# Later loads of k and v, rounding steps in turns for the second channel weight, and a closed joint, in a fused attention and mixer kernel

## The chip, the cores and the metric

The kernel runs on one core of a Trainium2 chip. Its engines are PE (TensorE, matmuls), DVE (VectorE), ACT (ScalarE), POOL (GpSimd) and SP (SyncE, which here issues nearly all DMAs). The metric is device time in microseconds, the median of several runs. Before the change it is 807.17 us (four runs, 806.99 to 807.58).

## The reference

All inputs of the attention are float32; the four weights of the mixer arrive in double precision and are rounded to float32 on the chip.

```python
# q, k, v: 8 batches, 8 heads, 576 rows, 64 columns
kv = einsum('bhsd,bhse->bhde', k, v)
out = einsum('bhsd,bhde->bhse', q, kv)
rms = sqrt(mean(out * out, axis=-1, keepdims=True) + 1e-06)
x = out / rms * g_norm                  # then to (8, 576, 512)
# mixer; w_tok1 576x256, w_tok2 256x576, w_ch1 512x1536, w_ch2 1536x512
h = maximum(x^T @ w_tok1, 0) @ w_tok2
u = x + h^T
h2 = maximum(u @ w_ch1, 0) @ w_ch2
result = u + h2
```

## The kernel before

The work has two parts. The **first pass** makes u = x + h for all eight batches, and rounds the weights on the side. The **second part** computes the channel mixing of u in nine groups of 512 rows (eight groups of the first 512 rows of a batch, and a ninth of the 64 remaining rows of each). Between the two u goes through DRAM (`u_dram`).

**First pass.** It works on pairs of batches, four pairs in all. Its order is written out by hand, as lists of names: `start` (attention of pair 0), `middle` (attention of pair 1, mixing of pair 0), `steady` twice (attention of pairs 2 and 3, mixing of pairs 1 and 2) and `last` (mixing of pair 3). `play` (L1059) runs a list from left to right, and each engine's queue follows that order. The names: `kv` products of k and v and `e` their eviction; `l00` to `l11` the loads of k and v for the next pair (`load`, L132: each issues two DMAs for k and two for v, on SP, into one of four pairs of buffers); `lq` the load of q; `a` the attention product of a chunk, `g` the product with g_norm (DVE), `q` the squares (ACT), `t` their sums (DVE), `m`, `r`, `i` the mean, root and inverse of the norm (DVE, ACT, DVE), `s` and `p` the scaling by the inverse (ACT or POOL); `h` the first token product, `z` the copy of x to PSUM as the start of a second token product, `u` the second token product with its eviction and the store of u. The two digits tell side or chunk and half.

A plain number in a list, such as `2`, runs that many steps of the **rounding** of the channel weights. A block of such a weight goes through eight functions: `fetch` (DMA of raw double words), `scale` (ACT), and six on DVE: clamp, shift, sign, power, lower and `both` (the sum of the two halves). `get_ch1` makes eight blocks of 128x768, `get_ch2` six of 128x1024. `stream` (L1048) puts the blocks behind each other, so that the six DVE steps of a block follow one another; the scale of the next block hangs on a block's fifth step (lower) and the fetch of the fourth block ahead on its sixth. Raw data has four buffers, the intermediate `part` one.

**Second part.** Both channel products use Strassen's scheme: seven products of halves in place of eight. In groups 1 to 8 it is applied twice over, with sums of weight blocks (`sums`) made once and kept in DRAM; `fetch_sums` brings them in, three ahead. Group 0 is done apart, with one level: `channel1_once` (matmuls into `ps_v`), then `channel2_once` (L703, into `ps_w`), while DVE makes the sums of the weights between its reads; `weave` spreads these over the products. The seven products of `channel2_once` stand in the order first, sixth, second, seventh, fifth, fourth, third. Fourth and third are read by DVE into the group's result `xg` and then stored.

Groups 1 to 8 are planned by place: `products[place]` holds one inner product, `beside[place]` what is issued after it. `outer` (L763) is one of the seven outer products, with seven inner ones at the places of `PLACE` (first at 0, sixth at 3, fifth at 4). After its first inner product ACT copies the bank `ps_a` to a bank `ps_c` of the pool "c" (two banks, `read_first`, L791), and the sixth product, which adds to `ps_a`, comes after that copy.

At the joint of group 0 and group 1 two matmuls whose result is not used stand around the first inner product (L1221 to 1224).

Of the kernel before, what the change touches and what calls it, by code (L numbers as in the profile page):

```python
# [11 lines left out]
F32 = mybir.dt.float32  # L12
# [7 lines left out]
def kernel(  # L20
# [33 lines left out]
    P = 128  # L54
    B, S, DM = k.shape
# [7 lines left out]
    NC, NF, NTOK = DM // P, DCH // P, DTOK // P  # L63
# [3 lines left out]
    FQ = FH // 2  # L67
# [31 lines left out]
    w_ch1 = consts.tile([P, 4, 4, FQ], F32, name="w_ch1")  # L99
# [6 lines left out]
    def do(f, *a, **kw):  # L106
        return lambda: f(*a, **kw)

    late = {}
# [454 lines left out]
    def fetch_x(g, i):  # L564

        if g < NG:
            if i == 0:
                xg[g] = late["xg"].tile([P, J, DM], F32, name="xg")
            dma(xg[g][:, ts(i, 2)], u_dram[g].rearrange("(t p) e -> p t e", p=P)[:, ts(i, 2)])
# [11 lines left out]
    blocks, blocks_dram = {}, {}  # L581
# [37 lines left out]
    def m_psum(shape, name):  # L619
        return late["m"].tile(shape, F32, name=name, tag="m")  # L620
# [82 lines left out]
    def channel2_once(g):  # L703

        shape = [P, 2, DH]
        x = xg[g]
        quarter = lambda i, j: x[:, 2 * i:2 * i + 2, ts(j, DH)]

        def product(n, ps, start, stop):
            for p in range(2):  # L710
                for s in range(NS):
                    matmul(ps[:, p], lhsT=late["once"][n - 1][:, s, p], rhs=w2_of(n)[:, s],
                           start=(start and p == 0 and s == 0), stop=stop,
                           skip_group_check=True)

        p1, p6, p7, p5 = (m_psum(shape, f"ps_w{n}") for n in (1, 6, 7, 5))
        t1, u2, u3 = (r_tile() for _ in range(3))

        def first():
            product(1, p1, True, False)  # L720
            copy(t1, p1)

        def sixth():
            product(6, p6, True, True)
            tensor_add(u2, p6, t1)

        def seventh():
            product(7, p7, True, False)
            tensor_add(u3, p7, u2)
            tensor_add(quarter(0, 1), quarter(0, 1), u2)  # L730
            tensor_add(quarter(1, 0), quarter(1, 0), u2)

        def fifth():
            product(5, p5, True, False)
            tensor_add(u3, p5, u3)
            tensor_add(quarter(1, 1), quarter(1, 1), u3)

        def second():
            product(2, p1, False, True)
            tensor_add(quarter(0, 0), p1, quarter(0, 0))  # L740

        def fourth():
            product(4, p7, False, True)
            tensor_add(quarter(1, 0), p7, quarter(1, 0))
            store(g, xg, 1)

        def third():
            product(3, p5, False, True)
            tensor_add(quarter(0, 1), p5, quarter(0, 1))
            store(g, xg, 0)  # L750

        return [first, sixth, second, seventh, fifth, fourth, third]
# [7 lines left out]
    def put(place, *steps):  # L760
        beside[place] += steps

    def outer(place, size, mul, to, base=None, act=copy, onto=False):  # L763

        banks, t = {}, {}

        def product(n, name, start, stop):
            if start:
                banks[name] = m_psum([P, size], f"ps_{name}")
            mul(n, banks[name], start, stop)

        def temp(n, bufs):
            t[n] = late["tmp"].tile([P, FQ], F32, name=n, tag=n, bufs=bufs)[:, :size]
            t[n] = fit(t[n])
            return t[n]

        def fit(flat):
            return flat if size == P else flat.rearrange("p (w t) -> p w t", w=W)

        def read(o, i, j):

            if base:
                tensor_add(o, fit(banks["a"]), base(i, j))
            else:
                copy(o, fit(banks["a"]))

        def read_first():  # L791
            banks["c"] = late["c"].tile([P, DM], F32, name="ps_c")[:, :size]
            read(fit(banks["c"]), 0, 0)

        def write(i, j, name, n):
            tensor_add(to(i, j), fit(banks[name]), to(i, j) if onto else t[n])

        def put_on(i, j, n):
            if onto:
                tensor_add(to(i, j), to(i, j), t[n])  # L800

        def take(i, j, name, act):
            if onto:
                tensor_add(to(i, j), banks[name], to(i, j))
            else:
                act(to(i, j), fit(banks[name]))

        def at(n, name, start, stop, *steps):
            def all_of():
                product(n, name, start, stop)  # L810
                for step in steps:
                    step()

            products[place + PLACE[n]] = all_of

        at(1, "a", True, False, read_first)
        at(6, "a", False, False, lambda: read(temp("u2", 2), 0, 1))
        at(5, "b", True, False)
        at(7, "a", False, False, lambda: read(temp("u3", 1), 1, 1))
        at(2, "c", False, True, lambda: take(0, 0, "c", act))  # L820
        put(place + PLACE[7] + (1 if onto else 2), do(put_on, 1, 1, "u3"), do(write, 1, 1, "b", "u3"))
        at(4, "a", False, True, lambda: take(1, 0, "a", copy) if onto else read(to(1, 0), 1, 0))
        put(place + PLACE[4], do(put_on, 0, 1, "u2"))
        at(3, "b", False, True)
        put(place + PLACE[3] + 1, do(write, 0, 1, "b", "u2"))
# [213 lines left out]
    def weave(body, fill):  # L1039
        done = 0  # L1040
        for n, step in enumerate(body):
            step()
            upto = len(fill) * (n + 1) // len(body)
            while done < upto:
                fill[done]()
                done += 1

    def stream(blocks, ahead=4):  # L1048


        steps = [blocks[0][1]]
        for n, block in enumerate(blocks):
            steps += block[2:]
            for at, m, k in ((-2, n + 1, 1), (-1, n + ahead, 0)):
                if m < len(blocks):
                    steps[at] = do(lambda *fs: [f() for f in fs], steps[at], blocks[m][k])
        return iter(steps)

    def play(lines, after={}, **stages):  # L1059

# [2 lines left out]
        for name in " ".join(lines).split():  # L1063
# [5 lines left out]
            else:  # L1069
# [6 lines left out]
    channel = ([get_ch1(c, f) for f in range(2) for c in range(NC)]  # L1076
               + [get_ch2(f) for f in range(NF // 2)])
# [20 lines left out]
    for block in tok1[2:] + tok2:  # L1098
# [11 lines left out]
        "h010 t21 m2 r2", "a30 g30 q30 i2 p20", "a31 g31 q31 t30", "h011 t31 m3 r3 p21", "a40 i3 p30 g40 q40 p31",  # L1110
        "h012 h013 t40 m4 r4 w21 i4 s40 lq0 l10 l11"]
    middle = [
        "kv00 e00 w31 w22 w23 w24", "h10 w25 w26 w27 f1 -lq1 l00 w32 w33 w34", "kv01 e01 l01 w41 w35 w36 w37",
        "h11 f2 w42 w43 w44", "hr w45 w46 w47 f3", "a0 q00 g01 q01 g00 t00 t01", "u0 z2 1", "u1 1",
        "a1 q10 g11 q11 g10 t10 t11 m0 r0", "u2 i0 1", "kv10 e10 z4 s00", "u3 1 s01", "kv11 e11 1",
        "u4 1 z6", "a2 q20 g21 q21 g20 s10", "u5 t20 t21 2", "a4 q40 g41 q41 g40 lq0 l10 l11", "u6 t40 t41 2",
        "a3 q30 g31 q31 g30 lq1 s11", "u7 t30 t31 m2 r2 1 i2 p20 p21 s30", "u8 1 s31"]

    def steady(n0, n1):
        return [  # L1120
            "kv00 l00 e00 1 -s40", "h00 3", "kv01 l01 e01 1", "h01 3", f"a0 q00 g01 q01 g00 {n0}",
            "h10 1 t00 t01 2", "h11 4", "hr 2 z2", "a1 q10 g11 q11 g10 1", "kv10 l10 e10 t10 t11 m0 r0 1",
            "u0 i0 1", "kv11 l11 e11", "u1 1 s00", "u2 z4 1", "a2 q20 g21 q21 g20", "u3 s01 t20 t21",
            "u4 z6 1", "a4 q40 g41 q41 g40 lq0", "u5 s10 t40 t41 1", "a3 q30 g31 q31 g30 lq1",
            "u6 s11 t30 t31 m2 r2 1 i2 p20 p21 s30", f"u7 1 s31 {n1}", "u8 2"]

    attentions = [attention(0, ((0,), (1,), (2,), (3,), (4,)))]
# [3 lines left out]
    mixings.append(token_mixing(B // 2 - 1, range(2, 9), (0, 1)))  # L1131
    more = {f"w{n}{k}": f for n, b in enumerate(tok1 + tok2) for k, f in enumerate(b)}
    more |= {f"f{n}": b[0] for n, b in enumerate(channel)}
    rounding = stream(channel)

    def keep_warm(n):

# [8 lines left out]
    for n in range(1, B // 2 - 1):  # L1146
        play(steady(*((3, 1), (0, 0))[n - 1]), attention=attentions[n + 1], mixing=mixings[n], before=attentions[n],
             rounding=rounding)
# [7 lines left out]
    first = ExitStack()  # L1156
# [46 lines left out]
    turns, loads = blocks1[1::2], blocks1[2::2]  # L1203
    n = len(sums1) // 3
# [8 lines left out]
             lambda: [f() for f in outer_u(1)], lambda: [f() for f in inner_u(1, 0, 7)]]  # L1213
    extra += [lambda: None] * (len(channel2_once_steps := channel2_once(0)) - len(extra))
    body = [step for pair in zip(channel2_once_steps, extra) for step in pair]
    weave(body, lasts + [f for fs, _ in inner2 for f in fs] + [f for _, f in inner1])
    fetch_x(1, 0)
    fetch_x(1, 1)


    for place in range(2):  # L1221
        t = late["c"].tile([P, DM], F32, name="ps_c")
        step = do(matmul, t[:, :FQ], lhsT=w_ch1[:, 0, 0, :P], rhs=w_ch1[:, 0, 0], start=True, stop=True)
        put(place, step) if place else step()
    for n, (_, f) in enumerate(inner2):
        put(8 + n, f)
    for g in range(1, NG):
# [42 lines left out]
```

## Time and profile before

The profile is of one execution, with times in microseconds from the start of its span.

| what | us |
|---|---|
| median of four runs | 807.17 |
| the profiled execution | 806.5 |
| its span | 804.7 |
| PE busy | 788.0 |
| DVE busy | 683.2 |
| ACT busy | 302.1 |
| POOL busy | 79.6 |
| `start` | 0 to 45 |
| `middle` | 45 to 79 |
| `steady`, first | 79 to 122.5 |
| `steady`, second | 122.5 to 167.6 |
| `last` | 167.6 to 199.3 |
| group 0, first channel product | 199.3 to 235.6 |
| group 0, second channel product | 235.6 to 271.9 |
| groups 1 to 8 | 273.9 to 804.7 |

In a line of a timeline the first number is the start, the second the length, then the engine, the line of the code, the operation, and output and input with shapes; "x4" means four instructions drawn together, and square brackets hold the idle time before them and what ended it. SPq is SP's DMA issue. The granted clock of TensorE was 0.999 over the span.

### The profile page before, as it was taken

The numbers are of one execution on the slowest core, as the hardware profiler recorded it, in microseconds if no ns is written. First come the engines' busy times: TensorE is split into PE (matmuls) and PEld (weight loads), VectorE is DVE, ScalarE is ACT, GpSimd is POOL, SyncE is SP. The second block draws the span as 40 slices with busy tenths as digits, with TensorE's granted clock in tenths as the row PEclk, the third lists the DMA queues.
The fourth block names the chain that finished last, engine by engine and source line by source line (L and its number), as shares of the span: only waits on it lengthen the run. The fifth ranks groups of instructions, "written<-read, shape, count | busy, mean of one in ns | idle before, by whom it ended". The sixth has DMA issues, their size and how long they took to land.

```text
span 804.7 us, 17651 instructions
## 1 busy us (share of the span) xinstructions
PE 788.0 (98%) x7012; PEld 694.0 (86%) x7012; DVE 683.2 (85%) x1308; ACT 302.1 (38%) x838; POOL 79.6 (10%) x75
## 2 busy tenths in 40 slices
PE   6999999999999999999999999999999999999997
PEld 6645545444888899999999999999999999999997
DVE  4688999999886978978987997897898899799687
ACT  1357585664210134234234234332424323423331
POOL 1210101010000021012003003001101200300300
PEclk9999999999999999999999999999999999999999
DMA  9999997436458567468457647738836855863642
GB/s 292 329 345 346 333 358 297 157 128 205 156 176 294 193 216 226 139 214 271 149 201 242 194 155 258 232 118 263 263 121 217 262 166 183 250 201 124 217 147 83
DMA packets 97346, 175.51 MB, mean 218 GB/s; under 512 B 7024, under 2 KB 54128, under 8 KB 97264
## 3 DMA queue, kind: packets, MB, share of 16 engines
q1 hardware_dynamic: 95584, 172.65, 65.7%
q10 hardware_dynamic: 1680, 1.74, 0.7%
q8 instruction: 55, 0.90, 0.5%
q14 instruction: 27, 0.22, 0.1%
HBM read 137.79 MB, written 36.57 MB: 217 GB/s over the span
## 4 chain that ended last, share of the span: by engine, by line
PE 83%; DVE 8%; DMA 4%; ACT 4%; issue 1%; SPq 0%; ACTq 0%; DVEq 0%
PE ps_a L127 37%; PE ps_b L127 19%; PE ps_c L127 9%; PE ps_v L127 5%; PE ps_w L127 5%; PE ps_u L127 3%; PE ps_h L127 3%; DMA v_in<-in_v_dram 2%; ACT x L475 2%; DVE x L421 1%; DVE ms L442 1%; DMA raw<-in_moe_w_ch_dram 1%; DMA k_in<-in_k_dram 1%; PE ps_o L127 1%; DVE part L187 1%; ACT sq L425 1%
## 5 line engine op out<-in xcount | busy, mean ns | idle before, releaser
L124 ACT COPY u<-ps_a 128x128 f32<-128x128 f32 (+1 forms) x160 | 56.1, 351 | 156.5 <-PE ps_a L127 156.5
L118 POOL TENSOR_TENSOR v<-v,v 128x384 f32<-128x384 f32 (+1 forms) x48 | 61.4, 1299 | 532.6 <-ACT v L124 492.8
L127 PE MATMUL ps_b<-uT,sums 128*128 128x128 f32 x672 | 86.2, 276 | 0.0
L127 PEld LDWEIGHTS ps_b<-uT,sums 128*128 128x128 f32 x672 | 80.7, 192 | 0.1
L118 DVE TENSOR_TENSOR v<-v,v 128x768 f32<-128x768 f32 (+1 forms) x86 | 79.4, 931 | 1.1
L127 PE MATMUL ps_a<-uT,w_ch 128*128 128x128 f32 x576 | 78.8, 275 | 0.0
L124 ACT COPY ps_c<-ps_a 128x128 f32<-128x128 f32 (+1 forms) x80 | 26.9, 336 | 129.5 <-PE ps_a L127 129.5
L118 DVE TENSOR_TENSOR v<-ps_b,u 128x384 f32<-128x384 f32 x112 | 61.6, 550 | 12.5 <-PE ps_b L127 10.7
L127 PEld LDWEIGHTS ps_a<-uT,w_ch 128*128 128x128 f32 x576 | 71.5, 192 | 0.4
L127 PE MATMUL ps_u<-h,w_tok 128*128 128x512 f32 (+1 forms) x160 | 68.0, 608 | 1.0 <-DVE w_tok L118 0.5
L127 PE MATMUL ps_h<-x,w_tok 128*128 128x512 f32 (+1 forms) x160 | 65.8, 604 | 0.0
L118 DVE TENSOR_TENSOR uT<-uT 128x512 f32<-128x512 f32 (+4 forms) x103 | 63.0, 628 | 0.8
L127 PE MATMUL ps_a<-uT,w 128*128 128x128 f32 x432 | 60.0, 275 | 0.0
L127 PEld LDWEIGHTS ps_a<-uT,w 128*128 128x128 f32 x432 | 54.0, 192 | 0.0
L127 PEld LDWEIGHTS ps_h<-x,w_tok 128*128 128x128 f32 (+1 forms) x160 | 25.9, 189 | 31.0 <-issue 28.3
L118 DVE TENSOR_TENSOR sv<-v 128x384 f32<-128x384 f32 x80 | 43.4, 550 | 10.4 <-ACT v L121 10.4
L127 PEld LDWEIGHTS ps_u<-h,w_tok 128*128 128x128 f32 (+1 forms) x160 | 24.5, 178 | 31.3 <-issue 24.9
L121 ACT ACTIVATE v<-v 128x384 f32<-128x384 f32 (+1 forms) x86 | 42.5, 527 | 23.0 <-DVE v L118 22.5
L118 DVE TENSOR_TENSOR xg<-xg,r 128x512 f32<-128x512 f32 x74 | 49.9, 685 | 0.7
L475 ACT ACTIVATE x<-x,inv 128x64 f32<-128x64 f32 x184 | 46.1, 337 | 9.6 <-DVE inv L461 9.6
L127 PE MATMUL ps_a<-sums,sv 128*128 128x128 f32 x336 | 47.0, 276 | 0.0
L127 PE MATMUL ps_a<-uT,sums 128*128 128x128 f32 x336 | 46.8, 275 | 0.0
(134 smaller groups left out, 1575.3 us busy)
## 6 DMA issues: line engine op xcount, KB each, us to landing
sums<-sums SPq DMA_DIRECT2D x112, 576.0 KB, 4.1
qT<-in_q_dram SPq DMA_DIRECT2D x8, 1152.0 KB, 9.7
xt<-u_dram SPq DMA_DIRECT2D x36, 256.0 KB, 3.7
blocks<-y SPq DMA_DIRECT2D x72, 128.0 KB, 2.6
uT<-blocks SPq DMA_DIRECT2D x36, 256.0 KB, 4.8
xg<-u_dram SPq DMA_DIRECT2D x18, 512.0 KB, 5.1
k_in<-in_k_dram SPq DMA_DIRECT2D x16, 512.0 KB, 9.2
u_dram<-x SPq DMA_DIRECT2D x16, 512.0 KB, 4.6
```

The source lines that it names most:

```text
L118: keep(engine.tensor_tensor(out=o, in0=a, in1=b, op=op))
L121: keep(nc.scalar.activation(o, a, AF.Relu))
L124: keep(nc.scalar.copy(o, a))
L127: keep(nc.tensor.matmul(*a, **kw))
L187: keep(nc.vector.scalar_tensor_tensor(out=part[0], in0=raw()[..., 0], scalar=2.0 ** -52, in1=part[0], op0=ALU.mult, op1=ALU.mult))
L421: keep(nc.vector.tensor_mul(x, bank[c, h], g_sb.to_broadcast([P, number(c), D])))
L425: keep(nc.scalar.activation(sq[c, h], bank[c, h], AF.Square))
L442: keep(nc.vector.tensor_reduce(stats_of(c)[0][:, h], sq[c, h], axis=AX.X, op=ALU.add))
L475: keep(nc.scalar.activation(x[:, k, h], x[:, k, h], AF.Copy, scale=inv[:, k, h]))
```

## The change

The lists get new places for the eight load steps of `middle` and `steady` (four names in each), one more rounding step at the end of `middle`, and `stream` gets an argument `turns`. Blocks below that number (the eight of the first channel weight) go as before. For the later ones (the second channel weight) the first three steps of a block alternate with the last three of the block before; the next block's scale hangs on the second step (shift), and the fetch of the fourth block ahead on the fifth (lower).

At the joint the two unused matmuls go. The last product of `channel2_once`, `third`, is taken out of the woven list and issued after the first inner product of group 1, followed by the two fetches of group 1's u. Two of the four PSUM banks of `channel2_once` now come from the pool "c", which `read_first` uses.

```diff
-        p1, p6, p7, p5 = (m_psum(shape, f"ps_w{n}") for n in (1, 6, 7, 5))
+        p1, p6 = (m_psum(shape, f"ps_w{n}") for n in (1, 6))
+        p7, p5 = (late["c"].tile(shape, F32, name="ps_c", tag="c") for _ in range(2))
...
-            banks["c"] = late["c"].tile([P, DM], F32, name="ps_c")[:, :size]
+            banks["c"] = late["c"].tile([P, DM], F32, name="ps_c", tag="c")[:, :size]
...
-    def stream(blocks, ahead=4):
+    def stream(blocks, turns, ahead=4):
+        def all_of(*fs):
+            return do(lambda: [f() for f in fs])
         steps = [blocks[0][1]]
-        for n, block in enumerate(blocks):
-            steps += block[2:]
-            for at, m, k in ((-2, n + 1, 1), (-1, n + ahead, 0)):
-                if m < len(blocks):
-                    steps[at] = do(lambda *fs: [f() for f in fs], steps[at], blocks[m][k])
-        return iter(steps)
+        second = []
+        for n in range(len(blocks)):
+            _, _, *first = blocks[n]
+            if n + 1 < len(blocks):
+                k = 1 if n >= turns else 4
+                first[k] = all_of(first[k], blocks[n + 1][1])
+            if n + ahead < len(blocks):
+                k = 4 if n >= turns else 5
+                first[k] = all_of(first[k], blocks[n + ahead][0])
+            if n < turns:
+                steps += first
+            else:
+                pairs = zip(first[:3], second or [None] * 3)
+                steps += [f for pair in pairs for f in pair if f]
+                second = first[3:]
+        return iter(steps + second)
...
     middle = [
-        "kv00 e00 w31 w22 w23 w24", "h10 w25 w26 w27 f1 -lq1 l00 w32 w33 w34", "kv01 e01 l01 w41 w35 w36 w37",
-        "h11 f2 w42 w43 w44", "hr w45 w46 w47 f3", "a0 q00 g01 q01 g00 t00 t01", "u0 z2 1", "u1 1",
+        "kv00 e00 w31 w22 w23 w24", "h10 w25 w26 w27 f1 -lq1 w32 w33 w34", "kv01 e01 w41 w35 w36 w37",
+        "h11 f2 w42 w43 w44", "hr l00 w45 w46 w47 f3", "a0 q00 g01 q01 g00 t00 t01", "u0 z2 1", "u1 l01 1",
         "a1 q10 g11 q11 g10 t10 t11 m0 r0", "u2 i0 1", "kv10 e10 z4 s00", "u3 1 s01", "kv11 e11 1",
-        "u4 1 z6", "a2 q20 g21 q21 g20 s10", "u5 t20 t21 2", "a4 q40 g41 q41 g40 lq0 l10 l11", "u6 t40 t41 2",
-        "a3 q30 g31 q31 g30 lq1 s11", "u7 t30 t31 m2 r2 1 i2 p20 p21 s30", "u8 1 s31"]
+        "u4 1 z6", "a2 q20 g21 q21 g20 s10", "u5 t20 t21 2", "a4 q40 g41 q41 g40 lq0", "u6 t40 t41 2 l10",
+        "a3 q30 g31 q31 g30 lq1 s11", "u7 t30 t31 m2 r2 1 i2 p20 p21 s30", "u8 2 l11 s31"]
     def steady(n0, n1):
         return [
-            "kv00 l00 e00 1 -s40", "h00 3", "kv01 l01 e01 1", "h01 3", f"a0 q00 g01 q01 g00 {n0}",
-            "h10 1 t00 t01 2", "h11 4", "hr 2 z2", "a1 q10 g11 q11 g10 1", "kv10 l10 e10 t10 t11 m0 r0 1",
-            "u0 i0 1", "kv11 l11 e11", "u1 1 s00", "u2 z4 1", "a2 q20 g21 q21 g20", "u3 s01 t20 t21",
-            "u4 z6 1", "a4 q40 g41 q41 g40 lq0", "u5 s10 t40 t41 1", "a3 q30 g31 q31 g30 lq1",
+            "kv00 e00 1 -s40", "h00 3", "kv01 e01 1", "h01 3", f"a0 q00 g01 q01 g00 l00 {n0}",
+            "h10 1 t00 t01 2", "h11 l01 4", "hr 2 z2", "a1 q10 g11 q11 g10 1", "kv10 e10 t10 t11 m0 r0 1",
+            "u0 i0 1", "kv11 e11", "u1 1 s00 l10", "u2 z4 1", "a2 q20 g21 q21 g20", "u3 s01 t20 t21",
+            "u4 z6 1 l11", "a4 q40 g41 q41 g40 lq0", "u5 s10 t40 t41 1", "a3 q30 g31 q31 g30 lq1",
             "u6 s11 t30 t31 m2 r2 1 i2 p20 p21 s30", f"u7 1 s31 {n1}", "u8 2"]
...
-    rounding = stream(channel)
+    rounding = stream(channel, 2 * NC)
...
     body = [step for pair in zip(channel2_once_steps, extra) for step in pair]
+    behind = body.pop(-2)
     weave(body, lasts + [f for fs, _ in inner2 for f in fs] + [f for _, f in inner1])
-    fetch_x(1, 0)
-    fetch_x(1, 1)
-    for place in range(2):
-        t = late["c"].tile([P, DM], F32, name="ps_c")
-        step = do(matmul, t[:, :FQ], lhsT=w_ch1[:, 0, 0, :P], rhs=w_ch1[:, 0, 0], start=True, stop=True)
-        put(place, step) if place else step()
+    put(0, behind, do(fetch_x, 1, 0), do(fetch_x, 1, 1))
```

## The prediction

> **What bounds the kernel now.** I read the engine totals first, then the chain of work that ended last, then busy time by stage.
>
> ```profile
> PE 788.0 (98%) x7012; PEld 694.0 (86%) x7012; DVE 683.2 (85%) x1308; ACT 302.1 (38%) x838; POOL 79.6 (10%) x75
> ...
> PE 83%; DVE 8%; DMA 4%; ACT 4%; issue 1%; SPq 0%; ACTq 0%; DVEq 0%
> ```
>
> PE (TensorE) is busy for 788.0 of 804.7 us, and holds 83% of the chain. Time can come only from PE work that goes away or from PE idle time. In the stages the columns are the stretch, its length, busy time of PE, weight loads, DVE, ACT and POOL, the granted clock, the DMA share and GB/s.
>
> ```profile
> 79.00:123.00 44.00, 43.73 (x544) 22.73 (x542) 40.62 (x71) 28.98 (x89) 2.79 (x2) 1.00 1.07 350
> 123.00:168.00 45.00, 43.56 (x519) 22.18 (x516) 42.90 (x66) 29.88 (x87) 2.39 (x2) 1.00 0.56 207
> 168.00:199.30 31.30, 31.30 (x81) 12.89 (x79) 30.92 (x38) 17.11 (x43) 3.05 (x2) 1.00 0.50 162
> ...
> 271.90:273.90 2.00, 2.00 (x11) 1.24 (x9) 1.93 (x5) 0.46 (x1) 0.00 (x0) 1.00 0.96 374
> 273.90:804.70 530.80, 526.11 (x4699) 525.65 (x4698) 452.27 (x916) 181.94 (x509) 61.45 (x48) 1.00 0.61 198
> ```
>
> The first two rows are the two `steady` stages, the third is `last`, the fourth the joint, the fifth the main loop, in whose timeline the 128x128 matmuls follow 112 ns apart without waits. So what is won ahead of 274 us reaches the end, if the main loop's transfers keep up. A busy PE is modelled, so I read stalls from starts: a group that starts later than its predecessor's count and pitch allow. By that count the steady stages lose 0.47 (109 to 111.3 us), 0.13, 0.2, 0.66 (152.8 to 155), 0.2 and 1.2 (to 161.04): 2.9 us. Their DVE is full and ends at 198.92, next to PE's 199.28; it decides when PE's inputs are ready.
>
> The timelines of SP, ACT, PE and DVE (start, length, what):
>
> ```profile
> 86.81 3.35 SPq L115 DMA_DIRECT2D v_in<-in_v_dram  x2
> 90.25 0.53 SPq L115 DMA_DIRECT2D raw<-in_moe_w_ch_dram  x1
> ...
> 99.17 0.94 ACT L163 ACTIVATE w_ch<-raw 128x768 f32<-128x768 f32 x1 [7.13 <-DMA raw<-in_moe_w_ch_dram]
> ...
> 103.08 0.69 DVE L421 TENSOR_TENSOR x<-ps_o,g_sb 128x512 f32<-128x512 f32 x1 [1.09 <-ACT sq L425]
> ...
> 161.04 1.16 PE L127 MATMUL ps_o<-kvp,qT 64*64 64x64 f32 x64 [1.12 <-ACT sq L425]
> ```
>
> A raw block, issued at 90.25 behind k and v, landed at 99.15. ACT waited 7.13 us, then DVE 1.09; PE had other work. The last line is PE's dearest stall.
>
> **The change part by part.**
>
> *Loads of k and v.* Eight steps move, each with four DMAs on SP (two for k, two for v; 5.6 us of SP between 84.51 and 90.25). In `middle` and `steady` each goes past rounding fetches and, for the second side, past stores of u; POOL's queue carries none of them. Ahead of the raw fetch they vanish, so it should land by 89 to 93 instead of 99.15: gain 0 to 1.09 us of DVE. The loss side is a late load: the tightest, the one of `kv11` at 103.0, now issues in the last row of `middle`, just before 79 us; with the median 9.2 us to landing and the raw fetch ahead it arrives by 93 to 96, 7 us early. Nobody waits soon for the u stores behind them. I take 0 for lateness; if the cover went, each later microsecond would be one of PE.
>
> *One more rounding step in `middle`.* Every step of `steady` is then one further, and `last` has one fewer. Its price on DVE is 0.55 (clamp) to 0.96 us (add, 110.11), ahead of `steady`. Against the 1.09 it leaves DVE 0.1 to 0.5 ahead. Following the DVE rows, the norm chain of the first steady stage ends about 0.65 us earlier, of 0.8 stall there. What is late next is DVE again.
>
> *Turns.* In the second weight the first three steps of a block alternate with the last three of the block before. A step that needs its neighbour's result starts later than one that doesn't:
>
> ```profile
> 143.25 0.69 DVE L183 TENSOR_SCALAR part<-w_ch 128x1024 uint32<-128x1024 uint32 x1
> 143.98 1.22 DVE L187 SCALAR_TENSOR_TENSOR part<-raw,part 128x1024 f32<-128x1024 uint32 x1
> 145.24 1.22 DVE L118 TENSOR_TENSOR w_ch<-w_ch,part 128x1024 f32<-128x1024 f32 x1
> ...
> 149.57 0.69 DVE L170 TENSOR_SCALAR w_ch<-w_ch 128x1024 uint32<-128x1024 uint32 x1
> 150.18 0.68 DVE L118 TENSOR_TENSOR x<-ps_u,x 128x512 f32<-128x512 f32 x1
> ```
>
> Dependent, 143.25 to 143.98 is 0.73, and 143.98 to 145.24 is 1.26; independent, 149.57 to 150.18 is 0.61. So 0.12 each; 18 such pairs stand between 132 and 199 us: 2.1 us of DVE. Only those ahead of 161 us can reach PE, some eight (1.0 us); the rest is slack in `last`, where PE has no stall (15.85 and 15.80 us for its two halves). And the new order puts sign and add (1.16 + 1.21) where clamp and shift (0.68 + 0.69) stood ahead of the reciprocals: 1.0 back. Row by row, the gain product of 146.38 comes 1.8 us earlier, but inv only 0.3, the seed copy 0.35 and the attention of 161.04 about 0.37 earlier than before, all told. So 0.37 of the first stage's 0.65 survives. Bounds for the first pass: −1.1 (0.65 and half of the second stage's stall that the heavier steps don't touch) and +0.6 (one heavy step, 1.21 less half, ahead of the norm chain). I take −0.37, by the rows.
>
> The Trainium skill, "VectorE: DVE Perf Modes", "The DRAIN you can't avoid", says that the next operation does not start until the pipe is empty, and that leaving out semaphores does not help (it adds that one that is not held starts earlier). By the flat rule turns save nothing, the 0.37 becomes about 0 and the sum −0.85; the rows above differ by 0.12, and I go by them.
>
> *The joint.* Two 128x384 matmuls go, and the last product of group 0 (24 records, 5.18 us) moves behind the first product of group 1.
>
> ```profile
> 271.08 0.68 DVE L118 TENSOR_TENSOR xg<-ps_w,xg 128x512 f32<-128x512 f32 x1
> ...
> 271.90 0.81 PE L127 MATMUL ps_c<-w_ch 128*128 128x384 f32 x2
> 272.55 0.83 PE L127 MATMUL ps_a<-uT,w_ch 128*128 128x128 f32 x6
> 273.22 0.81 PE L127 MATMUL ps_c<-w_ch 128*128 128x384 f32 x2
> 273.42 0.46 ACT L124 COPY ps_c<-ps_a 128x384 f32<-128x384 f32 x1 [31.75 <-PE ps_a L127]
> 273.93 0.94 PE L127 MATMUL ps_a<-uT,sums 128*128 128x128 f32 x6
> ...
> 274.97 0.39 SPq L115 DMA_DIRECT2D out_dram<-xg  x1
> ...
> 278.26 0.90 SPq L115 DMA_DIRECT2D xg<-u_dram  x2
> 280.42 0.33 SPq L115 DMA_DIRECT2D sums<-sums  x1
> ```
>
> The matmuls cover ACT's copy and cost 0.65 (271.90 to 272.55) and 0.71 (273.22 to 273.93): 1.36 at most. With them gone PE could go on at 273.93 − 1.36 = 272.57. But the copy now writes the bank that held the fourth product, and must wait for DVE's read of it, at 271.08 before and one sv operation (0.6) later now: it ends near 272.35; copy 0.46 and handover give 272.93, a gain of 1.0. The next copy into that pair of banks waits for the third product's read, now four fills later on DVE (near 276.1 to 276.8): copy and product at 277.37 where 278.22 stood. Net −0.85.
>
> The store of xg's first half then issues near 276.85, not 274.97; the fetch of the next xg waits for it to land (3.0 to 3.24 us) and issues near 280.0, not 278.26, and the sums behind it on SP near 280.9. They landed at 287.15 before (6.7 us, the sums' slowest; median 4.0) and PE used them at 287.60. Now PE wants them at 286.75. The bulk of xg and sums (1.64 MB at some 390 GB/s, 4.2 us), 1.6 from issue to full rate (278.3 to 279.9) and 0.3 to the signal put landing at 286.0: no stall. With before's 8.9 us from xg's issue to landing it is 288.9: 2.15 of stall. An instruction fetch of 2.69 us held one DMA engine then, so I take the first value and keep the second for a rival.
>
> **Sum.** −0.37 − 0.85 = −1.22 us. The profiled execution took 806.5 (span 804.7, 1.8 around it), the median of the four is 807.17, 0.67 above. So 805.3 profiled, 805.9 as a time.
>
> **The rivals.**
> - *Late sums (slower).* The joint's 0.85 turns into 2.15 − 0.85 = +1.3: with −0.37, 808.1; with the bad end of the first pass (+0.6), 809.1. It decides when xg's fetch issues after about 280.6 or an engine is held as at 279.56. For it: 0.45 us of slack before, less now. Against: the 6.7 us is one of 112 issues with median 4.1.
> - *Everything gives (faster).* Fourth's read comes in time, joint −1.36; first pass −1.1: 804.7, and with all 2.9 of steady stall gone 802.9. For it: ACT's 7.13 us and the turns leave DVE with 3 us less. Against: the norm chain has heavier steps ahead.
> - *The first pass gives nothing.* ACT's 7.13 us was hidden from PE anyway, and the extra step eats what DVE regains: −0.85 alone is 806.3, with +0.6 it is 806.9.
>
> **How the numbers follow.** Chances: the forecast 0.50 (own range 804.9 to 806.7), everything gives 0.24, nothing from the first pass 0.13, late sums 0.13. 0.2% is 1.6 us, about what a measurement of this kernel tells from no change: the bounds are 805.56 and 808.78. Faster: 0.20 of the forecast's half and 0.24, 0.44. Slower: the upper part of the late sums, 0.08. Same: 0.48. The range leaves out the end of 'everything gives' and of the late sums: 803.9 to 808.3.
>
> **What would show it.** ACT's wait near 92 us gone or under 1 us; the 18 dependent neighbours fewer; PE's stall before the attention near 161 about 1.2, the attention 0.3 to 0.4 earlier; the two 128x384 matmuls gone and the sixth product within 0.4 us of the end of the moved one; sums landing before PE's third outer product. I am wrong if that product waits for DMA, if a k or v load ends a wait of PE, or if PE's stall near 161 is gone altogether.

## The result, and the profile after

The changed kernel takes 805.94 us (median of 33 runs, 805.18 to 807.82), the kernel before 807.33 us (51 runs, 806.16 to 808.95). The ratio is 0.9982, with a 95% interval of 0.9978 to 0.9987: 1.05 to 1.78 us less. The prediction was 805.9. The total is right; the experiments show that the timed runs get it from other parts than the sum said. The profiled execution of the kernel before, against which all traces are read here, took 806.5 us, 0.8 less than this median of 807.33, and the one of the changed kernel 806.2, 0.2 above its own: the two traces differ by less than the medians do.

The page of the changed kernel: busy time by engine, and shares of the chain that ended last.

```profile
PE 785.8 (98%) x7008; PEld 692.3 (86%) x7008; DVE 681.9 (85%) x1308; ACT 301.9 (38%) x838; POOL 79.4 (10%) x75
...
PE 82%; DVE 8%; DMA 5%; ACT 2%; issue 1%; SPq 1%; DVEq 0%; ACTq 0%
```

Busy time by stage in the changed kernel, the two steady stages and `last` (stretch, length, PE, weight loads, DVE, ACT, POOL, clock, DMA share, GB/s):

```profile
79.00:123.00 44.00, 44.00 (x570) 23.46 (x565) 41.43 (x73) 29.31 (x90) 2.79 (x2) 1.00 0.98 319
123.00:168.00 45.00, 43.23 (x496) 21.66 (x491) 42.71 (x66) 30.74 (x88) 2.79 (x2) 1.00 0.66 237
168.00:199.30 31.30, 31.30 (x81) 13.06 (x80) 29.59 (x36) 16.29 (x43) 2.52 (x2) 1.00 0.53 167
```

ACT's share of the chain fell from 4 to 2%. The first steady stage shows PE without a gap; the second does not gain (43.23 busy, 43.56 before); in the stretch of `last` DVE is busy 1.3 us less. The stall of the first stage, in PE's timeline before and after, at the same matmuls:

```profile
111.26 1.98 PE L127 MATMUL ps_u<-h,w_tok 128*128 128x512 f32 x4 [0.20 <-ACT ps_u L124]
```

```profile
109.13 3.70 PE L127 MATMUL ps_u<-h,w_tok 128*128 128x512 f32 x8
```

Before, the four matmuls that start at 111.26 stand apart from the four ahead of them (109.07); in the changed kernel the eight follow one another without a gap.

The late raw block, in the timelines of SP and ACT of the changed kernel:

```profile
83.03 0.34 SPq L115 DMA_DIRECT2D raw<-in_moe_w_ch_dram  x1
83.42 1.12 SPq L115 DMA_DIRECT2D k_in<-in_k_dram  x2
...
91.62 1.73 ACT L163 ACTIVATE w_ch<-raw 128x768 f32<-128x768 f32 x2
98.02 0.60 ACT L121 ACTIVATE h<-ps_h 128x512 f32<-128x512 f32 x1 [4.66 <-PE ps_h L127]
```

The raw block is issued ahead of k and v, at 83.03 instead of 90.25, and lands at 91.39 instead of 99.15. ACT's wait of 7.13 us for it is gone; it now waits for PE.

PE and DVE in the second steady stage of the changed kernel:

```profile
148.69 1.22 DVE L118 TENSOR_TENSOR w_ch<-w_ch,part 128x1024 f32<-128x1024 f32 x1
149.82 0.68 DVE L118 TENSOR_TENSOR x<-ps_u,x 128x512 f32<-128x512 f32 x1
150.42 0.34 DVE L456 RECIPROCAL inv<-root 128x32 f32<-128x32 f32 x1
...
154.66 1.98 PE L127 MATMUL ps_u<-h,w_tok 128*128 128x512 f32 x4 [0.61 <-ACT ps_u L124]
...
160.66 1.16 PE L127 MATMUL ps_o<-kvp,qT 64*64 64x64 f32 x64 [1.12 <-ACT sq L425]
```

The rounding's add of 1.22 us now stands ahead of the reciprocal, and PE waits 0.61 where it waited 0.25, and again 1.12. The last line is the one that stood at 161.04. The wait of 0.25, in PE's timeline of the kernel before:

```profile
155.02 1.98 PE L127 MATMUL ps_u<-h,w_tok 128*128 128x512 f32 x4 [0.25 <-ACT ps_u L124]
```

The joint, in the timelines of PE, DVE, ACT and SP of the changed kernel:

```profile
267.01 5.35 PE L127 MATMUL ps_c<-w_ch,v 128*128 128x256 f32 x24
271.29 0.68 DVE L118 TENSOR_TENSOR xg<-ps_c,xg 128x512 f32<-128x512 f32 x1
272.06 0.46 ACT L124 COPY ps_c<-ps_a 128x384 f32<-128x384 f32 x1 [30.78 <-DVE xg L118]
272.58 0.94 PE L127 MATMUL ps_a<-uT,sums 128*128 128x128 f32 x6 [0.22 <-ACT ps_c L124]
275.64 0.68 DVE L118 TENSOR_TENSOR xg<-ps_c,xg 128x512 f32<-128x512 f32 x1
276.35 0.39 SPq L115 DMA_DIRECT2D out_dram<-xg  x1
279.38 0.88 SPq L115 DMA_DIRECT2D xg<-u_dram  x2
280.36 0.42 SPq L115 DMA_DIRECT2D sums<-sums  x1
286.40 0.83 PE L127 MATMUL ps_a<-uT,sums 128*128 128x128 f32 x6
```

PE does the moved product (24 matmuls) while DVE reads the fourth and ACT copies; only 0.22 us of waiting is left before the sixth product. The sums issued at 280.36 landed at 286.16, 0.24 us before PE used them.

Against the same matmuls before, PE stands at +0.11 us at 98.66 (start-up differs between executions by that much and more), at −0.73 at 117, at −0.39 from 157 to 235, at −1.36 at the sixth product, at −1.19 from 280 to 497, and at −0.55 at the end. The loss of 0.64 lies in the main loop. Its largest piece, in the timelines of DVE and PE of the changed kernel:

```profile
496.30 0.77 DVE L590 STREAM_TRANSPOSE y<-xt 128x256 f32<-128x256 f32 x2 [0.47 <-DMA xt<-u_dram]
...
497.56 0.94 PE L127 MATMUL ps_a<-uT,w_ch 128*128 128x128 f32 x6 [0.17 <-DVE u L118]
```

A transfer of xt landed 0.47 us late for DVE, the read of `ps_a` behind it on DVE came late, and PE lost 0.44 us by 499.

### The profile page after: what moved, and what is told of

Same layout as the page of the kernel before. It is cut to its first block, busy times and chain, and to the rows that moved or that the text cites. A ratio compares the mean times of both kernels' runs of the same rounds, so it can differ in the third digit from the quotient of the medians.

```text
span 804.4 us, 17644 instructions
## 1 busy us (share of the span) xinstructions
PE 785.8 (98%) x7008; PEld 692.3 (86%) x7008; DVE 681.9 (85%) x1308; ACT 301.9 (38%) x838; POOL 79.4 (10%) x75
## 4 chain that ended last, share of the span: by engine, by line
PE 82%; DVE 8%; DMA 5%; ACT 2%; issue 1%; SPq 1%; DVEq 0%; ACTq 0%
PE ps_a L127 37%; PE ps_b L127 18%; PE ps_c L127 10%; PE ps_v L127 5%; PE ps_u L127 4%; PE ps_h L127 4%; DMA v_in<-in_v_dram 2%; PE ps_w L127 2%; DMA raw<-in_moe_w_ch_dram 1%; ACT x L475 1%; DVE ms L442 1%; DVE x L421 1%; DMA k_in<-in_k_dram 1%; PE ps_o L127 1%; DVE part L187 1%
```

## The experiments

All ratios are against the kernel before, timed beside each batch of kernels (its median there was 807.33 to 807.67 us), with their 95% intervals; kernels of different batches are compared by these ratios. "Position" is the start of a matmul against the same one in the profile of before.

**The parts alone.** The first pass without the joint: the lists, `stream` and its call as in the change, everything from `channel2_once` on as before.

```diff
-    def stream(blocks, ahead=4):
+    def stream(blocks, turns, ahead=4):
...
-        "a3 q30 g31 q31 g30 lq1 s11", "u7 t30 t31 m2 r2 1 i2 p20 p21 s30", "u8 1 s31"]
+        "a3 q30 g31 q31 g30 lq1 s11", "u7 t30 t31 m2 r2 1 i2 p20 p21 s30", "u8 2 l11 s31"]
...
-    rounding = stream(channel)
+    rounding = stream(channel, 2 * NC)
```

> Only the edits of the first pass (places of the loads, one more rounding step in middle, turns); the joint as before. Theory, from the two traces: PE's position against before is 0.8 us better after the first steady stage and 0.4 us better from 161 us on, so the median is 0.4 us lower than before (0.9995). Rival, the first pass is where the whole change gains: 1.4 us (0.9983). Rival, the gain at 161 us is a chance of the one profiled execution: 0, and the attention near 161 stands within 0.1 us of before's 161.04.

806.41 us, 0.9987 (0.9979 to 0.9996): 1.0 us, of which the theory had expected 0.4. In the trace the position goes from +0.36 at 74 us to −0.48 at 117 and −0.15 from 157 on: 0.51 won. Trace and theory agree; the median shows more, though the interval reaches from 0.3 to 1.7 us. One reason for more is seen next, in the kernel that keeps the old first pass and has only the new joint:

```diff
-        p1, p6, p7, p5 = (m_psum(shape, f"ps_w{n}") for n in (1, 6, 7, 5))
+        p1, p6 = (m_psum(shape, f"ps_w{n}") for n in (1, 6))
+        p7, p5 = (late["c"].tile(shape, F32, name="ps_c", tag="c") for _ in range(2))
...
+    behind = body.pop(-2)
...
+    put(0, behind, do(fetch_x, 1, 0), do(fetch_x, 1, 1))
```

> Only the joint; the first pass as before. Theory: the sixth product stands 0.97 us earlier against the start of ps_v than before (74.65 us after it), the product near 286 us 0.8 us earlier, and the median is 0.8 us lower (0.9990). Rival, late sums give it back in most executions: the product that uses them waits for DMA, and the median is 0 to 1.3 us above before. Rival, the two removed matmuls were pure cost: 1.36 us lower.

807.49 us, 0.9999 (0.9990 to 1.0008): nothing to be told from no change. Yet its sixth product stands 73.68 us after the start of `ps_v`, 0.97 us sooner than before's 74.65, and 0.80 is left near 290 us, as expected. Two things in its trace eat it. In the old first pass the raw block came later still; ACT and PE of this kernel:

```profile
100.28 0.95 ACT L163 ACTIVATE w_ch<-raw 128x768 f32<-128x768 f32 x1 [7.61 <-DMA raw<-in_moe_w_ch_dram]
...
102.25 1.99 PE L127 MATMUL ps_u<-h,w_tok 128*128 128x512 f32 x4 [0.48 <-ACT h L121]
```

With ACT held 1.1 us longer than in the profile of before, PE did lose 0.48. In the profiles of the four kernels with the old lists (before, the turns alone, the two matmuls out, this one) the block landed at 99.15, 99.44, 99.39 and 100.26, and, measured by position from 99 to 109 us, PE lost at most 0.1 us there in the first three and 0.5 in the last. So the profile of before had caught a cheap case; how often the dear one comes is not shown. And in the main loop this execution lost 1.0 us.

The two unused matmuls taken out, and nothing else:

```diff
-    for place in range(2):
-        t = late["c"].tile([P, DM], F32, name="ps_c")
-        step = do(matmul, t[:, :FQ], lhsT=w_ch1[:, 0, 0, :P], rhs=w_ch1[:, 0, 0], start=True, stop=True)
-        put(place, step) if place else step()
```

> Before without the two unused matmuls of the joint, and the last product of group 0 left where it was. Theory: they filled a wait that is still there. The first inner product then starts at 271.90, its six matmuls end near 272.6, ACT copies 0.46 us and the sixth product starts 0.5 to 0.6 us after the first one's end, near 273.2: 0.7 us earlier than 273.93 and 0.3 us behind the closed joint. Rival, the moved product is not needed at all: the sixth product at 272.6 and 1.36 us lower. Rival, without the filling matmuls the clock or the pipeline suffers: a granted clock under 0.99 in this stage, and no gain.

806.78 us, 0.9990 (0.9981 to 0.9999): by time 0.8 us, where the closed joint alone gave 0.1, with intervals that overlap. PE and ACT of this kernel:

```profile
272.18 0.83 PE L127 MATMUL ps_a<-uT,w_ch 128*128 128x128 f32 x6
273.05 0.46 ACT L124 COPY ps_c<-ps_a 128x384 f32<-128x384 f32 x1 [31.11 <-PE ps_a L127]
273.57 0.94 PE L127 MATMUL ps_a<-uT,sums 128*128 128x128 f32 x6 [0.55 <-ACT ps_c L124]
```

With the first matmul out, the product group starts as soon as the one before ends; the second one had covered ACT's copy, and without it PE waits 0.55 to 0.7 us. The position moves from +0.28 to −0.37: 0.65 won, two thirds of what the closed joint wins, and the clock stays at 1.0. Moving the last product of group 0 into that wait is worth the other 0.3 there, of which 0.15 is left from 280 us on. In the main loop this profile loses 0.6 us near 696.

**Which edit of the first pass.** Loads only, `stream` as before:

```diff
-            "kv00 l00 e00 1 -s40", "h00 3", "kv01 l01 e01 1", "h01 3", f"a0 q00 g01 q01 g00 {n0}",
+            "kv00 e00 1 -s40", "h00 3", "kv01 e01 1", "h01 3", f"a0 q00 g01 q01 g00 l00 {n0}",
...
-        "a3 q30 g31 q31 g30 lq1 s11", "u7 t30 t31 m2 r2 1 i2 p20 p21 s30", "u8 1 s31"]
+        "a3 q30 g31 q31 g30 lq1 s11", "u7 t30 t31 m2 r2 1 i2 p20 p21 s30", "u8 1 l11 s31"]
```

> Before with the new places of the k and v loads, nothing else. Theory: the raw block lands in time, ACT's 7.13 us of wait near 92 us goes, DVE's 1.09 us of idle goes, and PE is about 0.3 to 0.5 us earlier at 117 us than before; from 161 us on 0 to 0.4 of it is left. Median 0.2 to 0.6 us lower (0.9995). Rival, the loads do it all: PE 0.8 us earlier at 117 us. Rival, a later load is late for its product: a wait of PE for k or v, and slower.

806.28 us, 0.9986 (0.9977 to 0.9995). Position −0.87 at 117 us and −0.78 from 168 on: the rival that the loads do it all. The rounding step only:

```diff
-        "a3 q30 g31 q31 g30 lq1 s11", "u7 t30 t31 m2 r2 1 i2 p20 p21 s30", "u8 1 s31"]
+        "a3 q30 g31 q31 g30 lq1 s11", "u7 t30 t31 m2 r2 1 i2 p20 p21 s30", "u8 2 s31"]
```

> Before with one more rounding step at the end of middle, nothing else. Theory: DVE spends the step (0.55 to 0.96 us) ahead of its full stretch and each stage has other steps at the numbered places; without the earlier raw block the wait of ACT stays. PE at 117 us within 0.3 us of before, median within 0.4 us. Rival, the step itself brings the 0.8 us at 117 us. Rival, it costs its 0.96 us on PE.

806.39 us, 0.9987 (0.9978 to 0.9996), position −0.83 at 117 us and −0.31 from 168 on: the theory is refuted in the stage; the median, 0.9 us lower, lies outside its 0.4 too, though the interval reaches it. A rounding step is more than an instruction on DVE; this one also issues the fetch of a raw block, which thereby goes ahead of the k load. The same ACT instruction in the kernels with the loads alone and with the step alone:

```profile
95.90 0.92 ACT L163 ACTIVATE w_ch<-raw 128x768 f32<-128x768 f32 x1 [3.89 <-DMA raw<-in_moe_w_ch_dram]
```

```profile
96.09 0.93 ACT L163 ACTIVATE w_ch<-raw 128x768 f32<-128x768 f32 x1 [3.66 <-DMA raw<-in_moe_w_ch_dram]
```

99.17 became 95.90 in one and 96.09 in the other, and either is early enough: PE's stall of the first stage is gone in both. The two do not add, since they take away one and the same wait. Turns only, with the new `stream` and the lists as before:

```diff
-    rounding = stream(channel)
+    rounding = stream(channel, 2 * NC)
```

> Before with the last weight's rounding steps in turns, nothing else. Theory: nothing changes ahead of 132 us; dependent neighbours of 1024 columns go from 18 to a few, 0.12 us each; the rounding ends about 2 us earlier on DVE in the last list, PE at 161 us is within 0.4 us of before (the steps ahead of the norm chain decide the sign), median within 0.4 us. Rival, the flat rule that a next operation always waits for an empty pipe: DVE starts no step sooner, and its last read is not earlier.

807.35 us, 1.0004 (0.9995 to 1.0013), position +0.41 at 74 us, +0.20 at 161 and +0.38 at 168: nothing. DVE does start sooner where neighbours do not depend: in the changed kernel's 1024-column steps 1.13 to 1.14 us from lower to the next instruction, 1.26 where the next one needs its result. Of the 18 pairs with the later start 5 are left, in the changed kernel and with turns alone; 13 at 0.12 are 1.6 us. But the theory of 2 us in the last list fails. The sums of `uT` follow the last rounding sum; in DVE's timelines of the kernel before, the changed kernel and the turns alone they start at

```profile
196.31 2.61 DVE L118 TENSOR_TENSOR uT<-uT 128x512 f32<-128x512 f32 x4
```

```profile
194.28 2.61 DVE L118 TENSOR_TENSOR uT<-uT 128x512 f32<-128x512 f32 x4
```

```profile
196.33 2.62 DVE L118 TENSOR_TENSOR uT<-uT 128x512 f32<-128x512 f32 x4
```

With turns alone that is 0.4 us sooner on before's clock (196.33 less the position of 0.38), and what was saved earlier did not reach this point. In the changed kernel it is 2.0 us, of which 0.4 is the earlier start of the stage (position −0.39) and 0.4 what the turns alone show; the other 1.2 us come from the rounding step that `last` no longer has: with the step alone the sums start at 194.73, by the same reckoning (position −0.31) 1.3 us sooner. All of it lies in `last`, where PE has no stall to lose. So the saving is real, smaller than counted, and buys nothing here.

**What limits the second stage.** The changed kernel, with the add of 1.22 us behind the inverse:

```diff
-            "h10 1 t00 t01 2", "h11 l01 4", "hr 2 z2", "a1 q10 g11 q11 g10 1", "kv10 e10 t10 t11 m0 r0 1",
-            "u0 i0 1", "kv11 e11", "u1 1 s00 l10", "u2 z4 1", "a2 q20 g21 q21 g20", "u3 s01 t20 t21",
+            "h10 1 t00 t01 2", "h11 l01 4", "hr 2 z2", "a1 q10 g11 q11 g10 1", "kv10 e10 t10 t11 m0 r0",
+            "u0 i0 2", "kv11 e11", "u1 1 s00 l10", "u2 z4 1", "a2 q20 g21 q21 g20", "u3 s01 t20 t21",
```

> The changed kernel, with the one rounding step that stands between the mean and the inverse of the norm in both steady stages moved behind the inverse. Theory: in the second stage this step is an add of 1.22 us ahead of the reciprocals; without it the inverse is 0.8 to 1.2 us earlier, the seed copy too, PE's stalls of 0.6 before 154.66 and of 1.1 before 160.66 shrink by 0.8 to 1.2 us together, and the median is 0.8 to 1.2 us below the changed kernel, near 804.9. Rival, the stall has another limit (the squares of the rest wait for DVE's reads, which the moved step now delays): under 0.3 us.

804.68 us, 0.9972 (0.9962 to 0.9981): by the ratios 0.8 us below the changed kernel, as the theory had it, with intervals that just touch. DVE and PE of it:

```profile
148.70 0.69 DVE L118 TENSOR_TENSOR x<-ps_u,x 128x512 f32<-128x512 f32 x1
149.30 0.34 DVE L456 RECIPROCAL inv<-root 128x32 f32<-128x32 f32 x1
...
155.77 0.76 PE L127 MATMUL ps_r<-kvp,qT 64*64 64x64 f32 x32
...
159.57 1.16 PE L127 MATMUL ps_o<-kvp,qT 64*64 64x64 f32 x64 [1.12 <-ACT sq L425]
```

The reciprocal starts 1.12 us sooner and the attention stands at 159.57 instead of 160.66. The stall of 0.61 is gone, the one of 1.12 stays. With the sign step moved too, half of that goes:

```diff
-            "h10 1 t00 t01 2", "h11 l01 4", "hr 2 z2", "a1 q10 g11 q11 g10 1", "kv10 e10 t10 t11 m0 r0",
-            "u0 i0 2", "kv11 e11", "u1 1 s00 l10", "u2 z4 1", "a2 q20 g21 q21 g20", "u3 s01 t20 t21",
+            "h10 1 t00 t01 2", "h11 l01 4", "hr 2 z2", "a1 q10 g11 q11 g10", "kv10 e10 t10 t11 m0 r0",
+            "u0 i0 3", "kv11 e11", "u1 1 s00 l10", "u2 z4 1", "a2 q20 g21 q21 g20", "u3 s01 t20 t21",
```

> The same kernel with the closed joint, and also the sign step (1.21 us in the second stage) moved from ahead of the sums of squares to behind the inverse. Theory: the inverse is another 1.1 to 1.2 us earlier, ACT's chain to the last squares starts earlier, and PE's last stall of 1.1 before the attention (159.57) shrinks; PE gains 0.4 to 1.1 us: near 804.0, 0.9958 to 0.9967. Rival: ACT was busy without a break from 150.5 to 158.7 there and its squares wait for the attention product before, so nothing moves: 0.9972. Rival: DVE now reads the token products too late for PE's banks, and it is slower than 804.68.

804.34 us, 0.9961 (0.9948 to 0.9975), the lowest ratio of all, and faster than both kernels. Its PE:

```profile
159.24 1.16 PE L127 MATMUL ps_o<-kvp,qT 64*64 64x64 f32 x64 [0.57 <-ACT sq L425]
```

From 74 us to the start of `ps_v` it wins 2.0 us on before, where the changed kernel wins 0.5 and the kernel with the norm first 1.5.

**The sums at the joint.** The changed kernel with the fetch of the next xg issued twice; `again` is that fetch into the same tile:

```diff
-    put(0, behind, do(fetch_x, 1, 0), do(fetch_x, 1, 1))
+    put(0, behind, *[do(again, i) for i in (0, 1, 0, 1)])
```

> The changed kernel with the fetch of group 1's xg issued twice, 1.05 MB more ahead of the sums of the third outer product. Theory: the sums land only 0.24 us ahead of their use in the changed kernel, so the 2.7 us that 1.05 MB take at 390 GB/s come out on PE: sums landing near 288.9, the third outer product waits about 2.5 us, and the median is 2.0 to 2.6 us above the changed kernel, 0.6 to 1.2 above before. Rival, the slack is larger than it looks or PE makes the wait up later: under 0.5 us above the changed kernel.

812.98 us, 1.0065 (1.0052 to 1.0077): some 7 us more than the changed kernel, where 2.0 to 2.6 were expected. The delay was larger than planned: SP issued the second pair only after the first had landed (282.85 and 284.19), and so the sums at 284.64 and not 280.36; they landed at 291.20, 5.0 us later than in the changed kernel. PE of this kernel:

```profile
291.33 1.62 PE L127 MATMUL ps_a<-uT,sums 128*128 128x128 f32 x6 [4.88 <-DMA sums<-sums]
292.74 2.77 PE L127 MATMUL ps_b<-uT,sums 128*128 128x128 f32 x12
```

The position goes from −1.31 to +3.74 at that product and to +6.07 at 290: the five microseconds of lateness are paid in full, and another 2.3 in the matmuls behind it. No matmul behind it waits; they are slow. The same 12 matmuls in the changed kernel:

```profile
287.07 1.50 PE L127 MATMUL ps_b<-uT,sums 128*128 128x128 f32 x12
```

The reason stands in the granted clock, here by stretch ahead of the wait and behind it (columns as in the stages above):

```profile
280.00:286.00 6.00, 6.00 (x56) 6.00 (x56) 4.14 (x9) 1.87 (x5) 0.00 (x0) 1.00 0.76 269
291.30:296.00 4.70, 4.67 (x22) 4.70 (x23) 0.45 (x1) 0.90 (x2) 0.00 (x0) 0.50 0.04 17
```

While PE waited, the clock of TensorE went from 1.00 to 0.50 (at 289.27, some 3 us after the last matmul had started) and came back at 296.09, 4.8 us after PE had resumed. In that time a matmul follows the one before after 213 ns instead of 112; 22 of them make the 2.3 us. So there is hardly any slack at this place (at most the 0.24 us between landing and use), and a wait this long is paid a second time by the clock.

The third product's read put ahead of five of the seven DVE fills, on the kernel with the norm first (whose own edit is the one shown above):

```diff
-    weave(body, lasts + [f for fs, _ in inner2 for f in fs] + [f for _, f in inner1])
-    put(0, behind, do(fetch_x, 1, 0), do(fetch_x, 1, 1))
+    fills = lasts + [f for fs, _ in inner2 for f in fs] + [f for _, f in inner1]
+    weave(body, fills[:-5] + [lambda: None] * 5)
+    put(0, behind, *fills[-5:], do(fetch_x, 1, 0), do(fetch_x, 1, 1))
```

> The kernel with the norm first and the closed joint; of the seven fills that DVE does between the reads of the fourth and the third product, five now come after the third's read. Theory: the third's read is about 2.3 us earlier, the store and the fetch of the next xg 2 us earlier, the sums of the third outer product land 2 us or more ahead of their use (0.2 before), the second copy waits no more, and PE gains 0.1 to 0.17 us: not to be told from the kernel with the norm first by time alone (0.9970 to 0.9972). Rival, late sums cost something in many timed executions: 0.3 us or more lower, and a smaller spread of the times. Rival, the fills that now come later are late for PE: a wait for them near 275 to 280 us.

804.69 us, 0.9967 (0.9955 to 0.9980). The sums land at 284.25 and PE uses them 1.46 us later; from the start of `ps_v` to the last matmul it takes 599.49 us against 599.65, the 0.16 expected. By time it is 0.4 us below the kernel with the norm first (0.9967 against 0.9972), far inside intervals of 1 us either way. Whether late sums cost something in other executions is not told from these runs.

Both edits together, the further move and the sooner read:

```diff
+            "u0 i0 3", "kv11 e11", "u1 1 s00 l10", "u2 z4 1", "a2 q20 g21 q21 g20", "u3 s01 t20 t21",
...
+    put(0, behind, *fills[-5:], do(fetch_x, 1, 0), do(fetch_x, 1, 1))
```

> Both edits together, on the kernel with the norm first. Theory: they do not touch, so the gains add: 804.68 less 0.4 to 1.1 less 0.1, near 803.8 (0.9957 to 0.9966). Rival: what is won ahead of 160 us runs into the same transfers, and it is no better than the better one of the two.

804.64 us, 0.9963 (0.9951 to 0.9976): no better than the further move alone, as the rival had it, though the interval holds the theory too. In its profile the first pass won 2.0 us again, and 0.8 went in the main loop near 498 us.

**What the closed joint is worth.** The kernel with the norm first, with the joint as before, the two unused matmuls and the banks `p7` and `p5` of the pool "m" included:

```diff
-    behind = body.pop(-2)
-    put(0, behind, do(fetch_x, 1, 0), do(fetch_x, 1, 1))
+    fetch_x(1, 0)
+    fetch_x(1, 1)
```

> The kernel with the norm ahead of the rounding step, but the joint as before (two unused matmuls, the last product of group 0 in its old place, fetches of xg behind it). Theory: the closed joint is worth 0.97 us to its sixth product and 0.8 us further on, so this is 0.8 us slower than the kernel with the norm first (0.9972 against before): 0.9982. Rival, as the joint alone measured: the closed joint is worth nothing in most executions because transfers in the main loop come late instead, and this is 0.9972 too.

805.49 us, 0.9975 (0.9965 to 0.9984), against 0.9972 with the closed joint: 0.25 us, with an interval that holds both the theory and the rival. The joint has thus three prices by time: 0.1 us alone, 0.4 (the changed kernel against the first pass alone), 0.25 here, each uncertain by more than its size. In the traces, from the start of `ps_v` to PE's last matmul:

| joint | us, by profile |
|---|---|
| as before | 600.45, 600.45, 600.44, 600.55, 600.63, 600.87 |
| closed | 599.65, 600.30, 600.66, 600.28 |
| closed, read sooner | 599.49, 600.30 |

In order the first row is before, first pass, turns, step, loads, and the norm first with the old joint; the second the norm first, the change, the joint alone and the further move. At its best a closed joint is 0.8 us shorter. But 4 of 6 profiles with it lose 0.6 to 1.0 us in the main loop, near 498 and 696 us, where loads of xt, xg and sums and stores of the turned blocks are under way together; 3 of 6 without it lose 0.1 to 0.4, one of them between 300 and 400 us and two near 498. The kernel with the two matmuls out, which has the old order of transfers, loses 0.6 us near 696.

The timed runs point the same way. In each pair that differs in the joint alone, the closed joint has the lower lowest time and the wider spread: 805.51 to 808.79 us (alone) against 806.03 to 808.53 (before, timed beside it), 805.18 to 807.82 (the changed kernel) against 805.87 to 807.01 (first pass alone; 33 runs against 11), 804.17 to 806.39 (norm first) against 805.18 to 806.49 (the same with the old joint). That fits executions of which some keep the gain and others lose it again. Whether closing the joint brings the waits about, by shifting transfers against each other, or only brings the main loop to these places earlier, or whether the profiles happened to fall so, stays open.

## Why the prediction was right, and where it was not

*Held, step by step.* The raw block was to land by 89 to 93: 91.39. No PE group of the steady stages waits for k or v, so lateness was rightly 0; the tightest load was issued only at 83.42, not just before 79, and its v landed by 95.49. The attention near 161 was to come 0.37 us earlier, with its stall still there: 0.38, stall 1.12. (From 74 us on it is 0.50, since this execution stood 0.11 late; the first stage won 0.84 and not 0.65, and the second lost 0.34 of it.) The heavier steps ahead of the norm were named as what eats the rest, and moving them won 1.0 and then 0.5 us. The sixth product was to start at 272.93 on before's clock; 272.58 plus the 0.39 that the stage is early is 272.97. The sums were to land at 286.0 (286.16), ahead of PE; that the time is so near is luck, since the fetch of xg was issued 0.6 us sooner than forecast (279.38, not 280.0) and issue to landing took 6.8 us and not 6.0. The 6.7 us that these sums took before were the slowest of three in that window, and not of all 112: two took longer, up to 7.3 us. The saving in `last` was rightly of no use, but it is not the 2.1 us of the count: the turns alone bring 0.4 there.

*The flat rule for DVE.* "VectorE: DVE Perf Modes", "The DRAIN you can't avoid", in the Trainium skill, taken flatly, gave the turns nothing. The rows show 1.13 against 1.26 us by dependence in the changed kernel too, so DVE does not behave by the flat rule; but the time of the turns alone (1.0004) is what the rule would have given, for another reason: what DVE saves does not reach a place where PE waits.

*Failed.* First, in the first pass: the size −0.37. Timed, the first pass alone is 1.0 us faster, and the loads alone and the step alone, which also bring the raw block sooner, measure the same (0.9986 and 0.9987); each interval by itself still reaches 0.4. The working took the stall of one profile as the stall of the kernel; an execution with the old lists in which the raw block came 1.1 us later lost 0.48 us more on PE. So the edit takes away a wait that varies. That this is where all of the difference comes from is not shown: it is one profile of four, and the profile of before lay 0.8 us under its median for reasons that the trace does not tell. Second, in the joint: −0.85 stood in the trace to 290 us, but the step "what is won ahead of 274 us reaches the end, if the main loop's transfers keep up" was used as if the condition held. It failed in four of the six profiles with the closed joint, and the timed gain of the joint is 0.1 to 0.4. The two errors are of opposite sign, which is why 805.9 came out: the total is right by luck. Third, the extra rounding step was priced as one DVE instruction; the raw fetch that it issues is what matters, and by it the step alone brings the whole gain of the first stage.

Among the rivals, late sums did not decide, but the doubled fetch shows that there was no slack beyond the 0.24 us. "The first pass gives nothing" is refuted by its interval (0.9979 to 0.9996).

## What to carry to other kernels

A wait that one profile shows as free can cost in the next execution: where an engine waited 7 us for a transfer, ask what one more microsecond of it would touch, and give the removal more than the one profile's stall. Where two edits take away the same wait, count it once, and count the DMA that a moved step issues before its arithmetic. Work that is spread over the gaps of a bound engine should stand behind the short chain that the matmuls wait for: here moving two instructions of 1.2 us took the ratio from 0.9982 to 0.9961, about as much as the whole change (1 to 0.9982).

## What the runs showed of the hardware that was not expected

A transfer that landed 5.0 us later in front of dense matmuls cost 7.4 us of PE: 5.0 of waiting, and 2.3 because the granted clock fell to 0.50 during the wait and stayed there for 4.8 us after it, with matmuls 213 ns apart and not 112. Waits of 0.2 to 1.1 us in the same traces left the clock at 1.00. And profiles of kernels with the same main loop differ by 0 to 1.0 us there; in the one followed to its cause, a load of xt landed 0.47 us late for DVE.
